# Loading keys by halves of the partitions in a talking-heads attention with two MLPs

## The chip, the cores and the metric

The kernel runs on one core of a Trainium2 chip. The metric is the device time of one execution in microseconds (us). A core has a TensorE for matrix products (PE for its products, PEld for loading their weights), a VectorE (DVE), a ScalarE (ACT), a GpSimd (POOL) and a SyncE (SP), which here issues all transfers between memory and the core. These engines run on their own and wait for one another by semaphores. Transfers are executed by 16 DMA engines.

## The reference

```python
def _attn_ref(q, k, v, w_pre, w_post):          # q, k, v: (4, 12, 448, 64)
    scale = 1.0 / np.sqrt(q.shape[-1])
    scores = scale * np.matmul(q, k.transpose(0, 1, 3, 2))
    scores = np.einsum('bhij,hg->bgij', scores, w_pre)
    scores = scores - np.max(scores, axis=-1, keepdims=True)
    attn = np.exp(scores)
    attn = attn / (np.sum(attn, axis=-1, keepdims=True) + 1e-09)
    attn = np.einsum('bhij,hg->bgij', attn, w_post)
    return np.matmul(attn, v)
# then x = (1792, 768), rows by token;  h = x @ w_in (768 x 2048)
# MLP 1: elu(h) @ w_out     MLP 2: relu(h)**2 @ w_out
```

There are 4 batches, 12 heads, 448 positions and 64 values a head. Scores are mixed over the heads before the softmax and again behind it. The two MLPs follow.

## The kernel before, in words

Products that need more than one pass of TensorE are done with values split in a high and a low part: a cast makes the high part, a subtraction the low part, and three products (high x high, high x low, low x high) are summed in PSUM.

*Attention.* The 448 query rows of a batch are cut in four chunks of up to 120 rows; 16 chunks in all. For a chunk, `scores` (L151) makes the scores of 12 heads in three calls of four heads (j = 0, 1, 2). It multiplies the split queries `qs` with the split keys `kh` and `kl` of heads in two row groups of TensorE, 64 partitions each, so that a key tile holds two heads one above the other: partitions 0 to 63 and 64 to 127. The scores go to the tile `sc`. A `gather` (L170) is a DMA that brings ten query rows of all 12 heads, 120 partitions, to a tile `graw`. There are 180 such groups. A group is split into `gh` (ScalarE, L178) and `gl` (GpSimd, L183), mixed over the heads by one product with a block matrix (`mix_pre`), its maximum is taken on VectorE (`nmax`), its exponentials on ScalarE (`ex`, L198), and `mix_post` (L220) mixes again and turns it. `values` (L245) multiplies with v.

*Order.* The order is written out by hand. The main loop has 90 steps; step m mixes two groups behind (`mix_post`) and two groups ahead (`mix_pre` of step m + 1), splits the groups of step m + 2 and gathers those of step m + 4. Other work is put beside a step by a table: a call of `scores` ("score step"), one of `values` ("value step"), or neither ("plain step"), and loads and splits of queries and keys. The keys of the next batch are loaded in three calls of `load_k`, two steps apart, each two steps ahead of its two calls of `split_k`, in the last chunk of batches 0, 1 and 2. `split_k` (L113) makes `kh` on ScalarE (L120) and `kl` on GpSimd (L121) for two heads, from the tile `kraw`, of which there are two.

*Start.* Batch 0's keys go to the tile `k_room`, all six loads one after the other on SyncE, behind the first chunk's queries (`q_room`) and ahead of three small loads (`both` twice, `rows`) and the second chunk's queries. VectorE does all splits there. When scores of the chunk are in `sc`, the first gathers start.

*SyncE* issues in order. Gathers, loads and stores of all kinds stand in its one row, and a gather waits there until a `graw` buffer is free.

*MLPs.* From about 500 us on, TensorE multiplies with weights that are loaded, converted and split ahead of their use.

Of the kernel before, what the change touches and what calls it, by code (L numbers as in the profile page):

```python
# [15 lines left out]
B, H, S, D = 4, 12, 448, 64  # L16
# [27 lines left out]
def bank(psum, tag):  # L44
    return psum.tile([128, 512], F32, name=f"ps_{tag}", tag=tag, bufs=BANKS[tag])


def attention(tc, psum, qr, kr, vr, w_pre, w_post, diagonal, xd, mlps):
    nc = tc.nc
    with ExitStack() as ctx:  # L50
# [54 lines left out]
        def load_k(b, j, raw=None):  # L105

            raw = early.tile([128, 2, S], F32, name="kraw", bufs=2) if raw is None else raw
            src = kr[b, :, 4 * j * S : (4 * j + 4) * S].rearrange("d (p a j) -> p a d j", p=2, a=2)
            for p in range(2):
                nc.sync.dma_start(out=raw[:, p, :], in_=src[p])  # L110
            kraw[b, j] = raw

        def split_k(b, p, hi_copy=nc.scalar.copy, engine=nc.gpsimd):  # L113
# [150 lines left out]
        for n in range(2, N):  # L264
            b, c = chunks[n]
            start = (first[n] - 2 * AHEAD) // 2 - 5
            for j in range(3):
                put(start + 2 * j, scores, n, j)
                busy.add(start + 2 * j)
            for i in range(2):  # L270
                put(max(0, start - 3 + 2 * i), load_q, n, i)
                put(start - 1 + 2 * i, split_q, n, i)
            if c == len(CHUNKS) - 1 and b + 1 < B:
                for j in range(3):
                    put(start - 3 + 2 * j, load_k, b + 1, j)
                    for p in range(2):
                        put(start - 1 + 2 * j, split_k, b + 1, 2 * j + p)
        for n in range(N):
            b, c = chunks[n]
# [31 lines left out]
        p = bank(psum, "post")  # L311
# [6 lines left out]
        for j in range(3):  # L318
            load_k(0, j, k_room[:, j])
# [403 lines left out]
```

## Time and profile before

| | |
|---|---|
| median of 3 runs | 1462.72 us (1462.32 to 1462.9) |
| the profiled execution | 1462.46 us, its span 1460.7 us |
| PE busy | 1409.3 us (96%) |
| PEld busy | 1261.0 us (86%) |
| DVE busy | 860.5 us (59%) |
| ACT busy | 673.3 us (46%) |
| POOL busy | 262.7 us (18%) |
| DMA queue of SP | 172.85 MB, 37.2% of 16 engines |
| chain that ended last | PE 86%, DMA 8% |

The busy time of an engine is the time in which its instructions ran; what matters is what it waits for in the stage concerned. The DMA share is the mean busy share of the 16 DMA engines, so one full engine is 0.0625. The granted clock is TensorE's, 1.00 being 2.4 GHz and 0.50 being 1.2 GHz.

### The profile page before, as it was taken

The numbers are of one execution on the slowest core, as the hardware profiler recorded it, in microseconds if no ns is written. First come the engines' busy times: TensorE is split into PE (matmuls) and PEld (weight loads), VectorE is DVE, ScalarE is ACT, GpSimd is POOL, SyncE is SP. The second block draws the span as 40 slices with busy tenths as digits, with TensorE's granted clock in tenths as the row PEclk, the third lists the DMA queues.
The fourth block names the chain that finished last, engine by engine and source line by source line (L and its number), as shares of the span: only waits on it lengthen the run. The fifth ranks groups of instructions, "written<-read, shape, count | busy, mean of one in ns | idle before, by whom it ended". The sixth has DMA issues, their size and how long they took to land.

```text
span 1460.7 us, 24184 instructions
## 1 busy us (share of the span) xinstructions
PE 1409.3 (96%) x8906; PEld 1261.0 (86%) x8906; DVE 860.5 (59%) x1929; ACT 673.3 (46%) x1505; POOL 262.7 (18%) x243
## 2 busy tenths in 40 slices
PE   4899999998999999999999999999999999999999
PEld 1777878886888899999999999999999999999998
DVE  2766766775778689976669888644442112444121
ACT  1656666765676566642235554315552112333111
POOL 0465555555555600000000000000000000000000
PEclk6899999999999999999999999999999999999999
DMA  1533443353363365554445557642122111111131
GB/s 58 166 117 109 144 135 127 121 164 109 105 203 132 123 199 164 175 182 155 147 142 158 162 186 227 195 135 61 52 65 66 58 41 44 55 55 55 44 103 39
DMA packets 104474, 174.40 MB, mean 119 GB/s; under 512 B 22339, under 2 KB 81827, under 8 KB 104355
## 3 DMA queue, kind: packets, MB, share of 16 engines
q1 hardware_dynamic: 104355, 172.85, 37.2%
q8 instruction: 70, 1.15, 0.3%
q14 instruction: 49, 0.40, 0.1%
HBM read 97.93 MB, written 36.18 MB: 92 GB/s over the span
## 4 chain that ended last, share of the span: by engine, by line
PE 86%; DMA 8%; issue 1%; SPq 1%; POOL 1%; ACT 1%; DVE 1%; POOLq 0%; ACTq 0%; DVEq 0%
PE ps_qk L577 11%; PE ps_qk L579 11%; PE ps_qk L578 11%; PE ps_post L220 8%; PE ps_post L579 5%; PE ps_mix L579 5%; PE ps_post L577 5%; PE ps_mix L578 5%; PE ps_post L578 5%; PE ps_mix L577 5%; PE ps_qk L245 4%; PE ps_qk L162 3%; DMA kraw<-kr 3%; DMA graw<-sc 2%; PE ps_mix L191 2%; PE ps_mix L189 2%
## 5 line engine op out<-in xcount | busy, mean ns | idle before, releaser
L468 ACT CAST wh<-wf 128x384 fp32r<-128x384 f32 (+1 forms) x240 | 126.6, 532 | 277.4 <-DVE wf L455 112.3
L183 POOL TENSOR_TENSOR gl<-graw,gh 120x448 fp32r<-120x448 f32 x178 | 202.8, 1144 | 212.0 <-ACT gh L178 206.0
L469 DVE TENSOR_TENSOR wl<-wf,wh 128x384 fp32r<-128x384 f32 (+1 forms) x238 | 137.3, 581 | 163.1 <-ACT wh L468 162.3
L220 PEld LDWEIGHTS ps_post<-wg,ex 120*112 120x112 f32 x1440 | 159.5, 180 | 23.1 <-DVE tot L204 8.1
L220 PE MATMUL ps_post<-wg,ex 120*112 120x120 f32 x1440 | 176.5, 276 | 1.7 <-ACT at L230 1.3
L198 ACT ACTIVATE ex<-ps_mix,nmax 120x448 f32<-120x448 f32 x180 | 113.3, 635 | 110.2 <-DVE nmax L196 107.3
L577 PE MATMUL ps_qk<-xh,wh 128*128 128x448 f32 x384 | 141.4, 368 | 0.0
L196 DVE TENSOR_REDUCE nmax<-ps_mix 120x1 f32<-120x448 f32 x180 | 110.6, 622 | 52.2 <-PE ps_mix L191 50.4
L578 PE MATMUL ps_qk<-xl,wh 128*128 128x448 f32 x384 | 141.3, 368 | 0.0
L579 PE MATMUL ps_qk<-xh,wl 128*128 128x448 f32 x384 | 141.3, 368 | 0.0
L227 DVE COPY at<-ps_post 112x480 f32<-112x480 f32 x162 | 105.4, 651 | 12.5 <-PE ps_post L220 12.5
L178 ACT CAST gh<-graw 120x448 fp32r<-120x448 f32 x180 | 99.8, 575 | 5.0 <-DMA graw<-sc 4.7
L165 ACT COPY sc<-ps_qk 120x448 f32<-120x448 f32 x179 | 82.7, 552 | 22.8 <-PE ps_qk L162 22.2
L189 PE MATMUL ps_mix<-gh,pre_l 120*120 120x448 f32 x180 | 76.2, 423 | 15.8 <-ACT ex L198 12.3
L615 DVE TENSOR_TENSOR tmp<-tmp 128x448 f32<-128x448 f32 x64 | 39.9, 623 | 77.6 <-ACT tmp L614 77.6
L245 PEld LDWEIGHTS ps_qk<-at,v 112*64 112x64 f32 x1536 | 75.7, 139 | 11.1 <-ACT gh L178 6.0
L245 PE MATMUL ps_qk<-at,v 112*64 112x110 f32 (+2 forms) x1536 | 83.6, 265 | 0.0
L579 PEld LDWEIGHTS ps_qk<-xh,wl 128*128 128x128 f32 x384 | 72.1, 188 | 7.4
L577 PEld LDWEIGHTS ps_qk<-xh,wh 128*128 128x128 f32 x384 | 72.1, 188 | 7.3
L578 PEld LDWEIGHTS ps_qk<-xl,wh 128*128 128x128 f32 x384 | 72.1, 188 | 7.2
L191 PE MATMUL ps_mix<-gl,pre_h 120*120 120x448 f32 x180 | 70.2, 390 | 8.4 <-POOL gl L183 7.8
L431 ACT ACTIVATE wf<-wd 128x384 f32<-128x384 f32 (+1 forms) x120 | 69.4, 579 | 15.1 <-DMA wd<-w1i 8.7
(136 smaller groups left out, 3185.2 us busy)
## 6 DMA issues: line engine op xcount, KB each, us to landing
graw<-sc SPq DMA_DIRECT2D x180, 210.0 KB
wd<-w1i SPq DMA_DIRECT2D x32, 384.0 KB
wd<-w1o SPq DMA_DIRECT2D x24, 512.0 KB
wd<-w2i SPq DMA_DIRECT2D x32, 384.0 KB
wd<-w2o SPq DMA_DIRECT2D x32, 384.0 KB
w1if<-wf SPq DMA_DIRECT2D x32, 192.0 KB
w1of<-wf SPq DMA_DIRECT2D x24, 256.0 KB
w2if<-wf SPq DMA_DIRECT2D x32, 192.0 KB
```

Source lines behind the costliest of these rows:

```text
L183: engine.tensor_tensor(lo, graw.pop(t), parts[t][0].bitcast(F32), ALU.subtract)
L189: nc.tensor.matmul(p, pre_l, hi, start=True, stop=False)
L196: nc.vector.tensor_reduce(nmax, p, AX.X, ALU.max, negate=True)
L198: nc.scalar.activation(e[-1], p, AF.Exp, bias=nmax, scale=1.0, accum_out=tot[:, t % 2 : t % 2 + 1])
L220: nc.tensor.matmul(p[:, c, :], e[:, c * NJ : (c + 1) * NJ], w, start=True, stop=True)
L227: nc.vector.tensor_copy(o, p)
L245: nc.tensor.matmul(p[64 * a : 64 * a + 64, k, :w], vt[b, i][:, jc, g * D : (g + 1) * D], at[n][:, jc, 6 * i + g, :w], start=(jc == 0), sto ...
L468: nc.scalar.copy(hi, f)
L469: (engine or nc.vector).tensor_tensor(lo, f, hi.bitcast(F32), ALU.subtract)
L577: mm(p, wh, xh, start=first, stop=False)
L578: mm(p, wh, xl, start=False, stop=False)
L579: mm(p, wl, xh, start=False, stop=last)
```

## The change

Four heads (j fixed) are 4 x 448 columns of `kr`, which has 64 rows. They are read as [p, a]: p the call of `split_k` that uses them, a the half of the partitions. Before, one load took p fixed: two heads, a = 0 and 1, to all 128 partitions, and its source has a as its first dimension. Now one load takes a fixed: p = 0 and 1 to 64 partitions, and its source has the 64 rows as its first dimension. Two loads of 224 KB remain, and the tile's contents are the same.

```diff
         def load_k(b, j, raw=None):
 
             raw = early.tile([128, 2, S], F32, name="kraw", bufs=2) if raw is None else raw
-            src = kr[b, :, 4 * j * S : (4 * j + 4) * S].rearrange("d (p a j) -> p a d j", p=2, a=2)
-            for p in range(2):
-                nc.sync.dma_start(out=raw[:, p, :], in_=src[p])
+            src = kr[b, :, 4 * j * S : (4 * j + 4) * S].rearrange("d (p a j) -> d a p j", p=2, a=2)
+            for a in range(2):
+                nc.sync.dma_start(out=raw[64 * a : 64 * a + 64], in_=src[:, a])
             kraw[b, j] = raw
```

A split of two heads (p) reads both halves of the partitions, so it now waits for both loads. `load_q` and `first_q` have the same form as the new loads already.

SyncE's row at the start of the program, as a difference (name, tile, partitions x rows x columns):

```order
 L719 UNCONDITIONAL_BRANCH
 L304 DMA q_room<-qr 64x6x120 x2
-L110 DMA k_room<-kr 128x1x448 x6
+L110 DMA k_room<-kr 64x2x448 x6
 L69 DMA both<-w_pre 120x1x12
 L69 DMA both<-w_post 120x1x12
```

Nothing moves; the six loads have another shape. SyncE's row in the first of the three places where the next batch's keys are loaded, in the changed kernel:

```order
L130 DMA qraw<-qr 64x3x120 x2
L110 DMA kraw<-kr 64x2x448 x2
L173 DMA graw<-sc 120x1x448 x4
L130 DMA qraw<-qr 64x3x120 x2
L110 DMA kraw<-kr 64x2x448 x2
L173 DMA graw<-sc 120x1x448 x4
L110 DMA kraw<-kr 64x2x448 x2
L173 DMA graw<-sc 120x1x448 x2
```

Here too the row is the one of before but for the shape of the key loads: a pair of them stands ahead of two or four gathers. On the other four engines the rows are the same, word for word.

## Rows read from the trace of the kernel before

**Rows 1.** DMA issues: tile<-source, queue, operation, count, KB of each.

```profile
kraw<-kr SPq DMA_DIRECT2D x18, 224.0 KB
```

**Rows 2.** Slices of 1 us: engines' busy time, granted clock, DMA share, GB/s.

```profile
3.00:4.00 1.00, 1.00 (x4) 0.44 (x3) 0.00 (x0) 0.00 (x0) 0.00 (x0) 1.00 0.95 237
...
5.00:6.00 1.00, 1.00 (x6) 0.29 (x3) 0.88 (x2) 0.00 (x0) 0.00 (x0) 1.00 0.08 32
6.00:7.00 1.00, 0.11 (x1) 0.00 (x0) 0.00 (x0) 0.00 (x0) 0.00 (x0) 1.00 0.13 50
...
41.00:42.00 1.00, 0.34 (x4) 0.00 (x0) 0.96 (x6) 1.00 (x4) 0.00 (x0) 1.00 0.65 251
```

**Rows 3.** SyncE's issues at the start (start, duration), then the six key loads' min/median/max.

```profile
0.73 1.43 SPq L304 DMA_DIRECT2D q_room<-qr  x2
2.21 18.37 SPq L110 DMA_DIRECT2D k_room<-kr  x6
20.62 3.62 SPq L69 DMA_DIRECT2D both<-w_pre  x1
24.30 1.97 SPq L69 DMA_DIRECT2D both<-w_post  x1
26.31 1.12 SPq L70 DMA_DIRECT2D rows<-diagonal  x1
27.48 2.35 SPq L304 DMA_DIRECT2D q_room<-qr  x2
...
L110 SPq DMA_DIRECT2D k_room<-kr x6: 542/3926/4554, 2.2 to 16.0; - x6
```

**Rows 4.** VectorE at the start: start, duration, instruction, idle before and its releaser.

```profile
5.05 0.35 DVE L137 CAST qsh<-q_room 128x360 fp32r<-128x360 f32 x1 [5.05 <-DMA q_room<-qr]
5.43 0.53 DVE L138 TENSOR_TENSOR qsl<-q_room,qsh 128x360 fp32r<-128x360 f32 x1
10.37 0.39 DVE L120 CAST kh<-k_room 128x448 fp32r<-128x448 f32 x1 [4.40 <-DMA k_room<-kr]
10.79 0.62 DVE L121 TENSOR_TENSOR kl<-k_room,kh 128x448 fp32r<-128x448 f32 x1
...
34.69 0.62 DVE L121 TENSOR_TENSOR kl<-k_room,kh 128x448 fp32r<-128x448 f32 x1
35.87 0.35 DVE L137 CAST qsh<-q_room 128x360 fp32r<-128x360 f32 x1 [0.56 <-DMA q_room<-qr]
```

**Rows 5.** Waits (total, times, longest), then one pair of key loads and its casts.

```profile
ACT kh L120 <- DMA kraw<-kr: 40.9, 15, 4.5
...
PE ps_mix L189 <- ACT ex L198: 12.3, 5, 3.6
...
81.23 5.12 SPq L110 DMA_DIRECT2D kraw<-kr  x2
...
94.06 0.57 ACT L120 CAST kh<-kraw 128x448 fp32r<-128x448 f32 x1 [1.92 <-DMA kraw<-kr]
...
98.66 0.56 ACT L120 CAST kh<-kraw 128x448 fp32r<-128x448 f32 x1 [4.03 <-DMA kraw<-kr]
```

**Rows 6.** Stretches: length, busy of PE, PEld, DVE, ACT, POOL; clock, DMA share, GB/s.

```profile
76.39:125.48 49.09, 43.65 (x371) 35.89 (x369) 30.02 (x82) 30.96 (x78) 27.92 (x26) 0.90 0.35 122
190.93:234.76 43.83, 39.87 (x347) 31.89 (x346) 27.56 (x75) 28.11 (x70) 25.58 (x24) 0.92 0.34 119
257.74:295.98 38.24, 37.62 (x370) 32.02 (x369) 29.63 (x82) 27.93 (x72) 21.06 (x20) 1.00 0.39 127
280.45:315.93 35.48, 34.86 (x348) 29.37 (x346) 27.59 (x76) 25.25 (x64) 19.20 (x18) 1.00 0.59 186
310.28:361.11 50.83, 43.01 (x371) 34.28 (x369) 29.58 (x82) 31.08 (x78) 27.95 (x26) 0.93 0.34 121
500.00:1460.70 960.70, 957.24 (x4906) 890.38 (x4904) 520.30 (x1022) 364.29 (x728) 3.31 (x4) 1.00 0.37 114
```

## The prediction

> **What bounds the kernel now.** I read the table of engines and the 40 slices first. TensorE is busy for 96% of the span, and from 500 us to the end it works 957.24 of 960.70 us at clock 1.00 [rows 6]. The keys are all used before that, so the change can gain nothing there by itself: whatever it saves before 500 us moves the rest forward whole. Next I read the DMA list and the DMA share in slices of 1 us. A key load carries 224.0 KB, and there are 18 of them beside the 6 of the start [rows 1]. While key loads alone are in flight the share of the 16 DMA engines is 0.13 at 50 GB/s [rows 2]. That is 2/16 = 0.125: two engines are full and fourteen are empty, at 25 GB/s each. The first query load, which already goes to 64 partitions at a time, shows 0.95 and 237 GB/s, and the gathers of score rows 0.65 and 251 GB/s, some ten engines at the same 25 GB/s each [rows 2]. So the width of a load, not memory, sets its speed.
>
> Then I read who waits. At the start, the issue of six key loads holds SyncE for 18.37 us [rows 3]: the first two take about 0.6 us each, the median is 3.93 [rows 3], since what was issued before has not drained. VectorE casts the first keys at 10.37 and ends the last subtraction at 34.69 + 0.62 = 35.31 us [rows 4]; between these it mostly waits, a load every 4.8 us. In the body, ScalarE waits 40.9 us for key loads in its kh casts, 15 times, and TensorE's waits for ScalarE's ex are the visible end of it [rows 5]. One pair of loads is issued from 81.23 us on, and its casts start at 94.06 and 98.66, after waits of 1.92 and 4.03 us [rows 5]. ScalarE works in order, so the exponentials, the gh casts and the score copies stand behind each such cast.
>
> **The change, part by part.** No instruction moves on any engine; each key load has the same bytes and the same place in SyncE's row, but goes to 64 partitions x 2 heads and not to 128 x 1. Its SBUF side is now laid out like the query loads, whose rows show 0.95 of all engines. A page of the Trainium skill states the rule behind this: DMA: Bandwidth & Descriptors, in Why a DMA increments its semaphore by 16 and not by 1, says that the slowest dimension of both access patterns decides how many of the 16 engines a load gets, so that a leading dimension of two gives two. By that rule the old source, which led with the pair of heads, gets two engines and the new one sixteen; the 0.13 and the 0.95 agree.
>
> One thing gets worse: the first head pair's split now needs both loads of a pair, where it needed one. At the new rate that is one more half pair, 0.6 to 1 us, and only the very first one at the start is exposed.
>
> *Start.* Key data begin to flow at about 5.36 us: the slice from 5 to 6 carries 32 of the steady 50 GB/s [rows 2]. A pair is 458,752 bytes. At the query load's 237 GB/s it takes 1.94 us, at 16 x 25 = 400 GB/s 1.15 us; these are my two ends, and I take the slow one, since it was measured on 64 partitions. Before, 229,376 bytes at 50 GB/s end at 5.36 + 4.59 = 9.95, and the cast starts 0.42 us later. So the first cast moves from 10.37 to 5.36 + 1.94 + 0.42 = 7.72 us. All six loads take 5.8 us at 237 GB/s and are there by 11.6, while the third pair is only wanted at about 12.9, so from 7.72 on VectorE is bound by its own work: six splits at 0.42 + 0.65 = 1.07 us [rows 4] are 6.42, and the one split of queries among them is 0.38 + 0.53 = 0.91. Its last subtraction ends at 15.05 instead of 35.31: 20.3 us earlier, or 21.0 with the fast rate. Before, it then waited until 35.87 for the second chunk's queries [rows 4]. If these no longer wait, another 0.56 us goes: 20.8 to 21.6.
>
> What may be late next is that query load. Before it SyncE issues three small loads for 3.62, 1.97 and 1.12 us [rows 3]. If they cost that by themselves, six key loads at no more than 0.72 us each (half of 1.43 for two [rows 3]) end at 6.5, the small ones at 13.2, the queries' issue at 14.7 to 15.6; the first query load was ready 2.89 us after its issue ended (0.73 + 1.43 to 5.05) [rows 3, 4], so these are ready at 17.6 to 18.5, and the gain shrinks to 35.87 - 18.5 = 17.4 us. Since these issue times fall in step with the key backlog, I think they are waits for room and take a value near the upper end: 20.5 us. Everything from there to the steady state is the same chain of dependent work and shifts whole.
>
> *Body.* Three stretches load keys for the next batch. I cut each at starts of the post matmuls of a step, and compare it with a stretch of exactly the same kinds of step that loads hardly any keys. The first and third (value, score, value, score, plain, score, score, value steps) take 49.09 and 50.83 us; the same eight steps without keys take 38.24 [rows 6]. The second (score, score, value, score, value, score, value) takes 43.83, and its like 35.48 [rows 6]. The excess is 10.85 + 12.59 + 8.35 = 31.8 us. It includes the stretches where TensorE runs at a lower granted clock, 0.90 to 0.93 on average against 1.00 [rows 6], which follow its idle times.
>
> Not all of that goes. The key splits themselves remain: six casts of 0.57 us on ScalarE and, on GpSimd, the difference of its busy times, 27.92 - 21.06 = 6.86 us a stretch [rows 6]. They have cover: in the like stretch ScalarE is busy 27.93 and GpSimd 21.06 of 38.24 us, so 10.3 and 17.2 us are free. But a plain step, the shortest of all, gets two key casts and two key subtractions beside its own work, and two score steps follow it, where ScalarE has most to do. The lower end is 0, the upper all of GpSimd's 6.86 us in each of three stretches, 20.6 us. I take 1.1 us a stretch, near the lower end because of that free time: 3.3 us. A load now needs 1 to 2 us of transfer, and the pair cited above was issued 12.8 us before its cast, so I expect no ScalarE wait for keys. Gain: 31.8 - 3.3 = 28.5 us.
>
> *Sum.* The profiled execution took 1462.46 us beside its span of 1460.7, and the median of the three timed ones is 1462.72, so nothing has to be scaled. 1462.46 - 20.5 - 28.5 = 1413.5 us.
>
> **The rivals.**
> *The splits take over.* ScalarE or GpSimd become the bound in the three stretches, once the keys come in time. For it: 26 operations of GpSimd take 27.92 us [rows 6], 1.07 each; a value step can hold two of keys, two of its own and one of queries, 5.4 us, while the eight steps of the like stretch last 38.24 / 8 = 4.8 us on average. Against it: the free time above, and the one step of lead that the lo parts have. With the whole 20.6 us: 1462.46 - 20.5 - 11.2 = 1430.8.
>
> *The second chunk's queries set the start.* The small loads cost what they show, and only 17.4 us are won there: 1462.46 - 17.4 - 28.5 = 1416.6.
>
> *No wider than before.* If a load to half of the partitions still gets two engines, a pair takes as long as it did; the last pair lands at about 34.3 us (0.42 ahead of the last subtraction [rows 4]) and both its splits come behind it, not one: 1.07 us at the start. In the body the first cast of a pair waits for the whole pair and the second no more: 0 to 2 us over nine pairs. 1462.46 + 1.07 + 0 to 2 = 1463.5 to 1465.5, no change that can be told. Against it: 237 GB/s for queries on the same 64 partitions. The Trainium skill has a rule that speaks for it: DMA: Bandwidth & Descriptors, Rules for kernel authors, says that two transfers to disjoint halves of the partitions serialize, and that one transfer over 128 partitions should be used instead. By that rule the edit wins nothing, which is this rival's time; the trace shows that the 128-partition load was the narrow one here, so I read the rule as one for loads of equal width.
>
> *Narrower, and slower.* The halves run below the 50 GB/s of before, which is the point from which this decides; at 25 GB/s, one engine's rate, a load takes 9.17 us and not 4.59. The six of the start end 27.5 us later, and the 1.07 comes on top; in the body each of nine pairs arrives up to 9.17 us later, 0 to 83 us. 1462.46 + 28.6 + about half of that = 1532. Nothing in the trace speaks for it but that no key load to 64 partitions is in it; the queries' 0.95 speaks against.
>
> **How the numbers follow.** The forecast, with its own range of 1408 to 1419: 0.76. Queries setting the start, 1416.6, lies in it or just above, to 1421: 0.08. Splits taking over, in part or whole, 1421 to 1431: 0.11. No wider: 0.03. Narrower: 0.01. A gain above the highest start and the whole excess (1462.46 - 21.6 - 31.8 = 1409.1) would need other waits to go too; below 1406 I see 0.01. The range 1406 to 1425 leaves out half of the splits' case and the last two rivals. A measurement tells about 0.2%, 2.9 us, from no change: faster 0.96, same 0.03, slower 0.01.
>
> **What would show it.** Right: the DMA share jumps above 0.5 behind the first queries; the issue of six key loads holds SyncE for some 4 us and not 18.37; the last key subtraction of the start ends near 15 us; ScalarE's waits for key loads are near zero; the three stretches take 39 to 40, 36 to 37 and 39 to 41 us at clock 1.00. Wrong: a share that stays at 0.13; VectorE waiting for the second queries after its last key split; TensorE waiting for gl or ex in the three stretches without any wait for keys; or, after 500 us, a part that is no longer as long as before.

## The result and the profile after

The changed kernel took 1408.91 us in the median of four executions (1392.54 to 1409.12), the kernel before 1462.52 (1461.26 to 1462.9). The ratio of the two is 0.9607 with a 95% interval of 0.9538 to 0.9676, some 57 us less. The forecast was 1413.5 and its range 1406 to 1425. The median lies in the range; the ratio, which counts the execution at 1392.54 with the rest, gives 1462.52 x 0.9607 = 1405.0, which is 1.0 below its low end. The profiled execution took 1409.12 us, its span 1407.3, 53.4 less than before. That span can be followed to its parts, and most of what follows does so. The execution at 1392.54 is a matter of its own.

The slices of 1 us at the start answer to [rows 2]; the columns are the same.

```profile
3.00:4.00 1.00, 1.00 (x4) 0.45 (x3) 0.00 (x0) 0.00 (x0) 0.00 (x0) 1.00 1.10 240
4.00:5.00 1.00, 1.00 (x4) 0.30 (x2) 0.00 (x0) 0.00 (x0) 0.00 (x0) 1.00 0.98 266
...
7.00:8.00 1.00, 0.16 (x2) 0.17 (x2) 0.58 (x2) 0.00 (x0) 0.00 (x0) 1.00 1.10 233
...
12.00:13.00 1.00, 0.91 (x8) 0.49 (x6) 0.97 (x3) 1.00 (x3) 0.00 (x0) 1.00 0.03 6
```

Where two engines moved 50 GB/s until about 33 us, all sixteen are now busy at some 240 GB/s (the share adds up packet times and can pass 1.00), and by 12 us nothing is left to load. SyncE's issues answer to [rows 3], VectorE's instructions to [rows 4].

```profile
2.21 3.87 SPq L110 DMA_DIRECT2D k_room<-kr  x6
6.12 0.90 SPq L69 DMA_DIRECT2D both<-w_pre  x1
7.07 0.78 SPq L69 DMA_DIRECT2D both<-w_post  x1
7.89 0.50 SPq L70 DMA_DIRECT2D rows<-diagonal  x1
8.44 1.34 SPq L304 DMA_DIRECT2D q_room<-qr  x2
```

```profile
7.39 0.39 DVE L120 CAST kh<-k_room 128x448 fp32r<-128x448 f32 x1 [1.05 <-DMA k_room<-kr]
7.82 0.63 DVE L121 TENSOR_TENSOR kl<-k_room,kh 128x448 fp32r<-128x448 f32 x1
...
13.46 0.63 DVE L121 TENSOR_TENSOR kl<-k_room,kh 128x448 fp32r<-128x448 f32 x1
14.00 0.34 DVE L137 CAST qsh<-q_room 128x360 fp32r<-128x360 f32 x1
```

Six key loads are issued in 3.87 us and not in 18.37, and the small loads behind them in 0.50 to 0.90, so most of their 3.62, 1.97 and 1.12 was not their own cost but waiting behind the key loads. VectorE works without a pause from the first cast to the second chunk's queries, whose cast starts at 14.00 us and not at 35.87. TensorE's waits, and one of the pairs of casts in the body, answer to [rows 5].

```profile
PE ps_mix L191 <- POOL gl L183: 6.2, 11, 0.6
PE ps_mix L189 <- ACT gh L178: 2.9, 2, 1.6
```

```profile
58.18 1.03 ACT L120 CAST kh<-kraw 128x448 fp32r<-128x448 f32 x2
```

The 12.3 us that TensorE waited for ex are gone from the list, and both casts of a pair run back to back with no idle time before them. ScalarE's 40.9 us for key loads have no row any more. The stretches, cut at the same steps as in [rows 6], and last the rest of the program from the first product of the MLPs on:

```profile
53.23:92.00 38.77, 38.16 (x370) 32.38 (x369) 29.95 (x82) 30.78 (x78) 27.67 (x26) 1.00 0.44 139
157.44:193.50 36.06, 35.40 (x347) 29.62 (x345) 27.69 (x76) 27.98 (x70) 25.62 (x24) 1.00 0.45 140
216.46:254.73 38.27, 37.65 (x371) 32.04 (x369) 29.63 (x82) 27.94 (x72) 21.05 (x20) 1.00 0.39 127
239.19:274.67 35.48, 34.86 (x347) 29.38 (x345) 27.59 (x76) 25.37 (x65) 19.20 (x18) 1.00 0.65 196
269.03:307.77 38.74, 38.12 (x370) 32.34 (x369) 29.94 (x82) 30.89 (x78) 27.64 (x26) 1.00 0.45 147
447.38:1407.30 959.92, 956.53 (x4899) 889.60 (x4897) 520.05 (x1021) 363.85 (x726) 2.60 (x3) 1.00 0.37 114
```

The same rest in the kernel before, from its first product of the MLPs on:

```profile
500.71:1460.70 959.99, 956.53 (x4899) 889.67 (x4897) 519.76 (x1021) 363.87 (x726) 2.60 (x3) 1.00 0.37 114
```

The three key stretches fell from 49.09, 43.83 and 50.83 us to 38.77, 36.06 and 38.74, at clock 1.00 throughout; their likes without keys stayed at 38.27 and 35.48. The first of them begins at 53.23 and not at 76.39: the start gave 23.16 us. The three stretches gave 10.32 + 7.77 + 12.09 = 30.18. Together that is 53.34 of the 53.4 us. In this execution the rest, 959.92 us, is as long as before, 959.99.

### The profile page after: what moved, and what is told of

Its sections match the earlier page's. It is cut to its first block, busy times and chain, and to the rows that moved or that the text cites. A ratio compares the mean times of both kernels' runs of the same rounds, so it can differ in the third digit from the quotient of the medians.

```text
span 1407.3 us, 24193 instructions
## 1 busy us (share of the span) xinstructions
PE 1388.7 (99%) x8906; PEld 1250.1 (89%) x8906; DVE 860.3 (61%) x1929; ACT 672.4 (48%) x1505; POOL 262.0 (19%) x243
## 4 chain that ended last, share of the span: by engine, by line
PE 93%; POOL 3%; issue 2%; DVE 1%; DMA 1%; ACT 1%; SPq 0%; POOLq 0%; ACTq 0%; DVEq 0%
PE ps_qk L577 11%; PE ps_qk L578 11%; PE ps_qk L579 11%; PE ps_post L220 10%; PE ps_mix L577 6%; PE ps_post L577 6%; PE ps_post L578 6%; PE ps_mix L578 6%; PE ps_post L579 6%; PE ps_mix L579 6%; PE ps_qk L245 5%; PE ps_qk L162 4%; PE ps_mix L191 2%; PE ps_mix L190 2%; PE ps_mix L189 2%; POOL gl L183 2%
## 5 line engine op out<-in xcount | busy, mean ns | idle before, releaser
L578 PE MATMUL ps_qk<-wl,hh 128*128 128x384 f32 x224 | 75.9, 339 | 0.0
```

Source lines behind the costliest of these rows:

```text
L578: mm(p, wh, xl, start=False, stop=False)
```

## The experiments

In the comparisons below a kernel is seldom one number: the kernel before, the changed one and each variant of the loads have executions about 16 us under their others. Sums of parts are made with the profiled execution.

**Start alone.** The six loads of the start by halves, the 18 of the body as before.

```diff
+            if b == 0:
+                src = kr[b, :, 4 * j * S : (4 * j + 4) * S].rearrange("d (p a j) -> d a p j", p=2, a=2)
+                for a in range(2):
+                    nc.sync.dma_start(out=raw[64 * a : 64 * a + 64], in_=src[:, a])
+            else:
+                src = kr[b, :, 4 * j * S : (4 * j + 4) * S].rearrange("d (p a j) -> p a d j", p=2, a=2)
+                for p in range(2):
+                    nc.sync.dma_start(out=raw[:, p, :], in_=src[p])
```

> Only batch 0's six key loads at the start go by halves of the partitions; the 18 in the body are as before. Theory (the width of the load, the two parts independent): the start is 23.2 us shorter, as the first eight steps of the two profiles stand to each other, and the three key stretches keep their 49.1, 43.8 and 50.8 us: 1439.3 us. Rival (the parts interact: what the start gains is given back at the first key stretch, whose loads meet it at another time): 1445 to 1462.

Three executions took 1439.26 to 1439.66 us and one 1423.93. The key stretches of the profiled one (1439.26; columns as in [rows 6]):

```profile
53.13:102.18 49.05, 43.39 (x370) 35.60 (x368) 30.02 (x82) 30.97 (x78) 27.90 (x26) 0.90 0.35 122
...
167.63:211.96 44.33, 39.49 (x347) 31.23 (x345) 27.54 (x75) 28.06 (x70) 25.61 (x24) 0.96 0.33 118
287.48:337.91 50.43, 43.81 (x370) 35.60 (x368) 29.70 (x82) 31.07 (x78) 27.96 (x26) 0.90 0.35 121
```

They begin 23 us earlier and last as long as they did. The start's gain is not given back.

**Body alone.** The same edit with `if b > 0`.

> Only the 18 key loads of the body go by halves; the six at the start are as before. Theory: the start keeps its length, the key stretches take 38.8, 36.1 and 38.7 us and the time is 30.2 us under before: 1432.3 us. Rival (parts interact): the two savings do not add up to 53.6, and this kernel lies above 1440 or below 1425.

Two executions took 1431.53 and 1433.19 us, two 1414.75 and 1415.09. The stretches of the one at 1433.19:

```profile
77.32:116.12 38.80, 38.18 (x370) 32.37 (x369) 29.95 (x82) 30.78 (x78) 27.68 (x26) 1.00 0.44 139
181.50:217.56 36.06, 35.40 (x348) 29.63 (x346) 27.68 (x76) 27.99 (x70) 25.65 (x24) 1.00 0.45 140
293.10:331.85 38.75, 38.13 (x370) 32.37 (x368) 29.94 (x82) 30.89 (x78) 27.69 (x26) 1.00 0.46 149
```

The start is long, the stretches are short. By the spans, start alone gives 1460.7 - 1437.5 = 23.2 us and body alone 1460.7 - 1431.4 = 29.3, together 52.5 of 53.4: the two parts are independent within 1 us. The missing 0.9 is time ahead of the first key stretch, which begins at 77.32 us here and at 76.39 before. The two at 1415 are below the 1425 that I had put down as a sign against that; the next experiments tell why they are not one.

**62 rows and 2 rows.** Halves of the partitions, all as in the changed kernel, but with a number of rows that has few divisors.

```diff
             for a in range(2):
-                nc.sync.dma_start(out=raw[64 * a : 64 * a + 64], in_=src[:, a])
+                for d0, d1 in ((0, 62), (62, 64)):
+                    nc.sync.dma_start(out=raw[64 * a + d0 : 64 * a + d1], in_=src[d0:d1, a])
```

> The same halves and the same two heads a load, but each half goes as 62 rows and 2 rows. If the number of engines is what counts, and a load gets as many as divide its first dimension, 62 rows get two engines: share 0.13, the start's loads again as slow as before, 1462 to 1470 us (1.07 us more than before at the start, and 24 more issues). Rival (what helps is that four heads go to one half at a time, or that rows of one head are read in another order): as the changed kernel, 1409 to 1414 us, with some 4 us of issue more at the start hidden.

Six of ten executions took 1476.32 to 1479.7 us, four 1458.55 to 1460.9. A slice at the start, SyncE's issue and VectorE's first cast and last subtraction of keys, from three views:

```profile
10.00:11.00 1.00, 0.00 (x0) 0.00 (x0) 0.00 (x0) 0.00 (x0) 0.00 (x0) 0.50 0.13 50
```

```profile
2.20 23.33 SPq L111 DMA_DIRECT2D k_room<-kr  x12
```

```profile
15.24 0.39 DVE L121 CAST kh<-k_room 128x448 fp32r<-128x448 f32 x1 [9.29 <-DMA k_room<-kr]
...
36.23 0.63 DVE L122 TENSOR_TENSOR kl<-k_room,kh 128x448 fp32r<-128x448 f32 x1
```

The share is 0.13 and the rate 50 GB/s again. So neither the halves nor the two heads that a load brings to each partition made the loads fast: 64 rows as the first dimension get sixteen engines, 62 get two. By the Trainium skill's page DMA: Bandwidth & Descriptors (Why a DMA increments its semaphore by 16 and not by 1) the largest number up to 16 that divides the slowest dimension of both access patterns counts, which is 2 for 62; the run agrees. The start ends 1.55 us later than before (36.86 against 35.31), but the span is 13.8 us longer than before, more than I expected. The three key stretches take 52.78, 49.62 and 54.50 us, 13.2 more than before together, and ScalarE's waits for keys rise from 40.9 to 53.0 us. I put that down to the first cast of a pair, which now waits for all of it. The six more issues of each stretch are another candidate, which no run rules out, though ScalarE's waits for gathers fell from 4.7 to 1.4 us.

**Quarters.** The two heads that one load brought before the change, as two loads of one head and 64 rows each: `for p in range(2): for a in range(2):` with `out=raw[64 * a : 64 * a + 64, p, :], in_=src[:, a, p]`.

> Two heads a load as before the change (p fixed), but each as two loads of 64 rows to 64 partitions, 112 KB, four for a tile where there were two. Theory (the first dimension of a load, and with it the number of engines, is all that counts): as wide as the changed kernel, first cast of keys earlier by about half a pair, 0.5 to 1 us, 1408 to 1410 us where the changed kernel has 1409. Rival (four heads a load, that is 3,584 bytes a partition and not 1,792, is what makes it fast): key loads take about twice as long a byte, the third pair is late at the start, 1412 to 1440.

Five of six executions took 1412.02 to 1413.82 us, one 1396.98. SyncE's issue and VectorE's wait at the start:

```profile
2.20 7.66 SPq L111 DMA_DIRECT2D k_room<-kr  x12
```

```profile
16.48 0.35 DVE L138 CAST qsh<-q_room 128x360 fp32r<-128x360 f32 x1 [3.49 <-DMA q_room<-qr]
```

The time of 1412 to 1414 us lies in the rival's range, yet its mechanism is not what made it. (A load of the changed kernel brings two heads, 3,584 bytes, to a partition; the rival's "four heads" are these.) The loads show shares of 0.60 to 0.69 at 158 to 197 GB/s from 5 to 11 us, and this is about what SyncE issues: 112 KB every 7.66 / 12 = 0.64 us are 180 GB/s. The three key stretches take 38.76, 36.05 and 38.72 us, as long as in the changed kernel, so there loads of one head serve as well. The first cast came at 5.94 us, 1.45 earlier. But twelve issues hold SyncE for 7.66 us, the second chunk's queries are issued late, and VectorE waits 3.49 us for them: late queries set the start, as in a rival of the prediction, though it is the key issues that make them late and not the small loads (0.92, 0.81 and 0.50 us). The first key stretch begins at 56.19 us, 3.0 later than in the changed kernel, and that is the whole loss.

**First pair in quarters, queries ahead of the small loads.** The version that this points to.

```diff
-            for a in range(2):
-                nc.sync.dma_start(out=raw[64 * a : 64 * a + 64], in_=src[:, a])
+            for p in ((0, 1), (1, 2)) if b == j == 0 else ((0, 2),):
+                for a in range(2):
+                    nc.sync.dma_start(out=raw[64 * a : 64 * a + 64, p[0] : p[1]], in_=src[:, a, p[0] : p[1]])
...
-        load_mixes()
         first_q(1)
+        load_mixes()
```

> The changed kernel, with its very first pair of key loads in quarters (two heads to 64 partitions each, those of the first split ahead) and the second chunk's queries issued ahead of the three small loads. Theory (at the start VectorE is bound by its own splits once the first two heads are there, and the queries must not be late): first cast at 5.9 us as with all loads in quarters and not at 7.4, no wait of VectorE for the second queries, everything behind 1.4 us earlier; 1407.5 us where the changed kernel takes 1408.9, and 1390.6 where it takes 1392.0. Rival (the end of the start hangs on ScalarE's score copies, which fill its time from 9.2 us on): gain under 0.5 us.

Two of six executions took 1407.37 and 1407.51 us, four 1391.09 to 1393.02. VectorE at the start of the one at 1407.51:

```profile
5.80 0.39 DVE L121 CAST kh<-k_room 128x448 fp32r<-128x448 f32 x1
...
9.30 0.40 DVE L121 CAST kh<-k_room 128x448 fp32r<-128x448 f32 x1 [0.57 <-DMA k_room<-kr]
...
13.25 0.34 DVE L138 CAST qsh<-q_room 128x360 fp32r<-128x360 f32 x1
```

The first cast is 1.6 us earlier than in the changed kernel, the second pair is 0.57 us late, and the span is 1405.7 against 1407.3. Of these 1.6 us the start's own share is about 1: the first step's post matmuls start at 25.25 us here and at 26.01 and 26.34 in two traces of the changed kernel, so the rival's 0.5 is passed. The rest is not shown to be the edit's, since the six steps behind took 26.47 us here and 27.22 and 26.61 there. The two longer executions lie 1.2 to 2.2 us under the changed kernel's longer ones (1408.74 to 1409.54 in two comparisons), but on another chip; the shorter ones straddle its 1391.96 to 1392.54. The ratio to the kernel before, 0.957 (0.9509 to 0.9631), can't be told from the changed kernel's.

**The changed kernel again: what the execution at 1392 was.**

> The changed kernel once more, five rounds. Of its four executions three took 1408.87 to 1409.12 us and one 1392.54; the profile is of one of the three. Theory A (a part that is the same in both kernels, the MLPs, ran faster in that one): then the kernel before shows such executions too, some 16 us below 1462, about one in four or rarer. Theory B (something that only the changed kernel has, its attention after the loads, can go two ways): then only the changed kernel shows them.

Three of six executions took 1391.96 to 1392.05 us and three 1408.74 to 1409.54. Of 17 of the kernel before, on the same chip, five took 1446.49 to 1447.63 and twelve 1462.3 to 1465.71. So it is in both kernels, and A holds. This time the profiled execution was one of the short ones (span 1390.3). First the changed kernel's profile shown above, then this one: every 448-column product of TensorE starts a row of the timeline, and these are the first and the last of 22 and of 19.

```profile
599.66 0.37 PE L577 MATMUL ps_qk<-hh,wh 128*128 128x448 f32 x1
...
604.00 0.37 PE L577 MATMUL ps_qk<-hh,wh 128*128 128x448 f32 x1
```

```profile
599.82 0.36 PE L577 MATMUL ps_qk<-hh,wh 128*128 128x448 f32 x1
...
603.42 0.36 PE L577 MATMUL ps_qk<-hh,wh 128*128 128x448 f32 x1
```

One started every 4.34 / 21 = 0.207 us there, and every 3.60 / 18 = 0.200 here, at clock 1.00 in both. I call this time from start to start the pace. The MLPs have 3456 such products. In the first trace all keep 0.2066 us in the mean; in the second the 2304 of the layers that read `xh` and `xl` keep 0.2027 and the 1152 that read `hh` and `hl` 0.2000. So 0.200 and 0.203 are one quick pace in two layers, and 2304 x 3.9 + 1152 x 6.7 ns make 16.7 us. The attention is the same within 0.4 us (the first product of the MLPs starts at 447.01 and not 447.38), and what follows is shorter:

```profile
447.01:1390.30 943.29, 939.82 (x4899) 890.74 (x4897) 519.57 (x1021) 363.76 (x726) 2.62 (x3) 1.00 0.37 116
```

It has the same instructions as the 959.92 us of the changed kernel's first profile.

**Idle stretches in the MLPs: what sets that pace.** Sixty needless copies on ScalarE in the middle of each of four stretches starve TensorE for 28 us.

```diff
                     for j, bl in enumerate(blocks):
                         activate(p[j], f, bl)
+                    if f == 8:
+                        pad = self.tmp()
+                        for k in range(60):
+                            nc.scalar.copy(pad, p[0])
```

> The changed kernel with 60 extra copies on ScalarE in the middle (f = 8) of each of the four stretches of 16 steps in the MLPs, some 34 us each, so that TensorE falls idle for about 20 us four times and its granted clock falls and rises again. It asks what sets the pace of the MLPs' 448-column products, which was 0.207 us in one profiled execution of the changed kernel and 0.200 to 0.203 in another. Theory A (the pace is set anew whenever the clock rises): the pace differs between stretches of one execution, with five stretches most likely both values in it. Theory B (the pace belongs to the execution as a whole): one pace in all five stretches. Time: 1392 or 1409 plus about 80 us, and in between by A.

It took 1515.01 and 1516.34 us, some 106 above 1409 and not 80, since TensorE was idle for 28 us each time and not for 20. Products 18 apart before the first idle stretch, the first product behind it, and products 18 apart behind that:

```profile
499.83 0.37 PE L577 MATMUL ps_post<-xh,wh 128*128 128x448 f32 x1
...
503.55 0.37 PE L577 MATMUL ps_post<-xh,wh 128*128 128x448 f32 x1
...
554.61 0.74 PE L577 MATMUL ps_mix<-xh,wh 128*128 128x448 f32 x1 [27.96 <-ACT wh L468]
...
569.78 0.36 PE L577 MATMUL ps_qk<-xh,wh 128*128 128x448 f32 x1
...
573.43 0.36 PE L577 MATMUL ps_post<-xh,wh 128*128 128x448 f32 x1
```

0.2067 us before and 0.2028 behind it, in one execution: the pace does not belong to the execution.

> The same kernel as the one with four idle stretches, for a second trace. A: stretches of both paces within the trace; B: one pace throughout, in this trace and in the other, whichever it is.

It took 1521.87 and 1526.89 us. Here 18 products took 3.72 us (0.2067) from 660.08 on, behind the first idle stretch, and 3.60 us (0.2000) from 1159.80 on, behind the third. A holds against B in both traces. Whether it needs the clock's fall, the short ones ask: the same edit with 14 copies at f = 3, 6, 9 and 12.

> The changed kernel with 14 extra copies on ScalarE, some 7.9 us, at f = 3, 6, 9 and 12 of each stretch of the MLPs: sixteen idle times of TensorE of about 2 us, in which its clock should stay at 1.00 (the 60 copies, 33.8 us, made 28 us of idle time). If it is the fall and rise of the clock that sets the pace of the 448-column products anew, the pace does not change at these short gaps: one value for like products from 460 us to the end. Rival (any stop of TensorE sets it anew): the pace changes at some of the sixteen gaps. Time: 1392 or 1409 plus about 32 us.

It took 1455.94 to 1465.98 us, the profiled one 1461.59, some 52 us above the changed kernel and not 32: the idle times were up to 4.7 us, and at some the clock did fall (0.69 from 519 to 530 us). At others it did not: the stretch from 968 to 1078 us, with three idle times in it, and products around the first of them:

```profile
968.20:1078.50 110.30, 104.05 (x505) 93.97 (x503) 42.03 (x77) 78.16 (x156) 0.00 (x0) 1.00 0.20 63
```

```profile
989.88 0.37 PE L577 MATMUL ps_qk<-xh,wh 128*128 128x448 f32 x1
...
993.60 0.37 PE L577 MATMUL ps_post<-xh,wh 128*128 128x448 f32 x1
...
1007.53 0.47 PE L577 MATMUL ps_mix<-xh,wh 128*128 128x448 f32 x1 [1.99 <-ACT wh L468]
...
1015.73 0.36 PE L577 MATMUL ps_qk<-xh,wh 128*128 128x448 f32 x1
...
1019.99 0.36 PE L577 MATMUL ps_qk<-xh,wh 128*128 128x448 f32 x1
```

The clock is 1.00 throughout, TensorE stands still for 1.99 us, and the pace goes from 0.2067 to 4.26 / 21 = 0.2029 us. So the clock theory falls, and the rival holds: a stop is enough. Not even a stop is needed. In the changed kernel's first trace the MLPs' first 36 products stand ahead of the last `values`, and the rest behind it:

```profile
448.07 0.36 PE L577 MATMUL ps_mix<-xh,wh 128*128 128x448 f32 x1
...
451.72 0.36 PE L577 MATMUL ps_mix<-xh,wh 128*128 128x448 f32 x1
...
454.85 4.66 PE L245 MATMUL ps_qk<-at,v 112*64 112x108 f32 x96
...
460.16 0.37 PE L577 MATMUL ps_qk<-xh,wh 128*128 128x448 f32 x1
...
463.88 0.37 PE L577 MATMUL ps_qk<-xh,wh 128*128 128x448 f32 x1
```

18 products take 3.65 us (0.2028) ahead of the 96 products of `values` and 3.72 (0.2067) behind them, and from 447.4 to 466 us TensorE is never idle and its clock is 1.00. The short execution keeps 0.203 across the same place.

> The same kernel with sixteen short gaps, for a second trace. Clock theory: one pace throughout, maybe another than in the first trace. Rival: changes at gaps while the clock stays at 1.00.

One execution, 1460.49 us. Its products took 0.2027 us before the first stop, 0.2067 behind the second and 0.2027 again behind the third: it changes at stops here as well. It also changed from 0.203 to 0.2066 across the 384-column products from 845 to 964 us, in which TensorE did not stop. What decides which pace a stream of products falls into when it starts, I did not find out.

## Why the prediction was right and where it was wrong

*The bound, and what the change does: right.* Two engines before, sixteen now; the 62 rows show that halves alone do not do it, and the quarters that one head a load is as good in the body.

*Start: 23.2 us, forecast 20.5.* The first cast came at 7.39 and not 7.72, the last subtraction ended at 14.09 and not 15.05. The rate was near the lower of the two ends, 220 to 266 GB/s in the slices from 4 to 9 us, as I had taken it; the 400 did not come. That the first cast agrees is partly luck. Keys flow from about 4 us on and not from 5.36, and from 4 to 7 us 266, 220 and 240 GB/s moved, 726 KB or the bytes of three loads, before the first two could be used: a start too late and a pair too short nearly cancel. The queries were not late, and their cast moved by 21.87 us, a little past my upper end of 21.6. The rest, 1.3 us, I had excluded by saying that everything behind "shifts whole". It does not: the scores of the second chunk ran at a clock of 0.54 from 36 to 39 us before, with 0.73 us for the longest of the products; they run at 1.00 and 0.37 from 14 to 17 us now. From the chunk's first product to the start of its last they took 4.60 us before (36.37 to 40.97) and 3.46 now (14.65 to 18.11), which is 1.1 of the 1.3.

*Body: 30.2 us, forecast 28.5.* The key splits cost 0.50, 0.58 and 0.47 us over the like stretches, 1.55 in all, where I had put 3.3. Their cover held. The other 30.2 of the 31.8 us of excess were the waits, with the clock that followed them.

*Rivals.* The splits did not take over. The second chunk's queries did not set the start, but with twelve key issues ahead of them they do (3.49 us). No wider than before: its price was mis-sized, since I gave the body 0 to 2 us, and in the kernel whose loads are no wider (62 rows) the three key stretches alone cost 13.2, for a span of 1474.5 against 1460.7.

*The step that failed.* "Whatever it saves before 500 us moves the rest forward whole", with the MLPs as a fixed 960.70 us: that was read from one execution. In the profiled execution of the changed kernel it held, and gave 1409 and not 1413.5, since both terms were too small by 4.4 us in sum, within the range. But from the first product of the MLPs on the program takes 959.9 or 943.3 us by the pace of its products, whatever the change, and one of the four executions had the short one. The sum had no term for 16.6 us, and the low end of 1406, just 3.1 us under the highest gain that I had worked out, no room for it. A part after 500 us that is not as long as before stood among the signs of being wrong, but without a price. Executions of like pace on one chip agree with the traces' 53.4 us within 2: the median of the longer ones falls from 1464.15 to 1408.84 us, that of the shorter ones from 1446.84 to 1392.03, 55.3 and 54.8 us.

## What to carry to other kernels

Read a load's width from the DMA share while it is alone in flight, in sixteenths: 0.13 is two engines, and a first dimension of 64 rows instead of two heads gave all of them, one of 62 two again. Where a transfer that an in-order engine waits for becomes quick, count the clock that the waiting had cost as well. And before a long stretch that keeps TensorE busy is carried over as a constant, look at it in more than one execution.

## What was not expected of the hardware

- A stream of 448-column products with new weights each time runs at 0.200 to 0.203 us (by the layer) or at 0.207 a product, at clock 1.00, and in these traces the pace changed only where something came between: a stop of 1.99 us, or 4.7 us of other products without a stop. The 384-column products kept 0.177 us in all traces.
- Sixteen engines moved 220 to 266 GB/s of keys with shares of 0.98 to 1.10, some 15 GB/s each, where two engines moved 50 GB/s, 25 each.
- Loads that were too narrow held up SyncE itself: 18.37 us for six issues on two engines, 23.33 for twelve (six of 62 rows, six of 2), against 3.87 for six on sixteen.
